# First stages of a two-layer state-space and attention kernel: a new order of the work, and row means by TensorE from transposed rows

## The chip, the cores and the metric

The kernel runs on one core of a Trainium2 chip. Its time is device microseconds (us) of that core. Five engines work side by side, each through its own instructions in order: PE (TensorE, matmuls; PEld is its weight loads), DVE (VectorE), ACT (ScalarE), POOL (GpSimd) and SP (SyncE, which here only issues DMAs). POOL and ACT issue DMAs too. Engines wait for one another, and for DMAs, through semaphores. An instruction that waits holds up all that stand behind it on its engine, DMA issues included.

## The reference

The input u (2048 rows of 512) passes through four blocks: a long convolution (A), a local attention (B), A again and B again, each on the normalised input, and with the input added.

```python
def _A_ref(u, A_re, A_im, B_re, B_im, C_re, C_im, log_dt, Dskip):
    dt = jnp.exp(log_dt)[:, None]
    P = jnp.exp((dt * A)[:, :, None] * l[None, None, :])
    K = jnp.einsum("dn,dnl,dn->dl", Cc, P, dB).real
    ...
    Yf = Uf * Kf[None, :, :, :]
    y = irfft2(Yf)[:, :, 0, :L].transpose + u * Dskip
...
x = A_u
x = x + _A_ref(_layernorm(x, axis=-1), ...)
x = x + _B_ref(_layernorm(x, axis=-1), B_wqkv, B_wo)
x = x + _A_ref(_layernorm(x, axis=-1), ...)
x = x + _B_ref(_layernorm(x, axis=-1), B_wqkv, B_wo)
```

`_layernorm` takes mean and variance of each row of 512. The kernel K of the convolution (2048 lags for each of 512 channels, from 128 modes) and its spectrum are the same in both A blocks and are computed once.

## The kernel before

`kgen` (L384) makes the kernel's spectrum, normalises the rows for the first time, makes the first stage of their transform, and runs the first convolution. All of it is written as small steps with names, and the string `KGEN` (L353) is the order in which they are issued, by hand: each engine gets its instructions in that order. `words` holds each step with the steps that it needs. The part behind the colon, or the first digit, is the quarter of the channels (0 to 3). The steps:

- q, m, l, b (L425 to L441): the ladder. Each rung squares the modes' decay factor (q on ACT, m and l on DVE), and b casts it to bf16 on ACT. x0 to x5 form C times B, and t loads an activation table.
- U and v (`step`, L460): products of table entries with ladder rungs, on DVE. Their pairs are added either on DVE (% steps, L510) or by PE with identity weights (+, `sum_pe`, L521) and a copy on ACT (=, `sum_out`, L531). u, A and B copy start values.
- p (`product`, L558): PE multiplies the two tables of a quarter into lags of the kernel. k (L575) copies them to SBUF, and after the second copy sends them to DRAM and back in another layout (`rows`).
- s (`spectrum`, L593): PE multiplies rows with the transform matrix G. G0 serves parts 0 and 1, G1 parts 2 and 3. o and e (L613, L627) take the result out on ACT and DVE and store it to `kt_scratch` in DRAM, two DMAs of 128 KB each.
- n (`first_norm_row`, L176): sums of one row group of X. On ACT (an a behind the number) that is a pass for the mean (L184) and a pass for the squares (L185). On DVE it is L179 to L181. r and a make scale and bias for eight groups, and N applies them, on ACT (with a, L202) or DVE (L204).
- f (`first_stage`, L633) is the first transform stage of a group on PE with the matrix F1, and z (L638) copies it to Z: whole on ACT, or real and imaginary halves on ACT and DVE.
- c0 to c2 (L660): the last lag. c1 is eight small matmuls on PE and the last reader of the ladder's powers. `C["powers_used"]` holds it.
- w and W with a number of columns (`warm`, L550): matmuls of the identity whose results nobody reads, as filler on PE.
- steps with @: the first convolution, 16 groups (`a_steps`, L211): T transposes on PE, t (or a) copies them on DVE (or ACT), X second stage, c copy on ACT, p (pab, DVE) the product with the spectrum tile Kt, v inverse on PE, V (or W) the copy on ACT (or DVE), k the load of a Kt. U and Y belong to the last lag. A d, q, i, I or J is the second half of the last group.

Kt has five buffers, of two halves of 256 KB each. What the steps behind T0 need from DRAM is placed by `tc.issue_after`: the load of F1T, the matrix of the output stage, right behind `C["powers_used"]`, and the first four Kt loads right behind the steps in `FIRST_LOADS`: two on POOL's queue, behind the last `rows` DMA, and two on SP's queue. `load_b_weights` (L149) also sets a tile `never` to zero on POOL (L152), in memory that G0 held, so it waits for the last read of G0.

X is loaded by four DMAs of 512 KB on SP; F1 (1 MB), G1 (1.5 MB) and then G0 (1.5 MB) follow on the same queue.

Of the kernel before, what the change touches and what calls it, by code (L numbers as in the profile page):

```python
# [11 lines left out]
ACT = mybir.ActivationFunctionType  # L12
# [163 lines left out]
def first_norm_row(nc, small, st, Xg, j, on_act):  # L176
# [7 lines left out]
    nc.scalar.activation(junk[:], x, ACT.Identity, scale=1.0 / D, accum_out=mv[:, 0:1])  # L184
# [131 lines left out]
def a_layer(nc, tc, C, Xg, Ng, kt_dram, layer, Z, es_z, a=None):  # L316
# [10 lines left out]
    def y_rows(g, hf, row, ps, add):  # L327
# [25 lines left out]
KGEN = ("m0 q0 b0 x1 l0 m1 q1 x0 t l1 b1 x3 x2 q2 m2 b2 l2 x5 m3 U4p:1 q3 U4:0 l3 b3 %U4:0 u:1 m4 q4 u:0 l4 b4 m5 q5 U2p:0 l5 +U2p:0 b5 "  # L353
# [30 lines left out]
def kgen(nc, tc, C, prm, kt_dram, Zf, norm_row, norm_rstd, norm_apply, norm_apply_row, norm_tiles, load_rest, es_a, es_y, open_conv):  # L384
    everything = KGEN.split()
    with ExitStack() as es:
# [32 lines left out]
        nc.sync.dma_start(Gt[1][:], C["G_h"].ap()[1])  # L419
# [89 lines left out]

        def sum_dve(name, c):  # L510
            prod, out, hn, f, size = sums[name, c]
            for r in range(2):
                x, y = (prod[i][:, (r + i) % 2].rearrange("n (h f c) -> n h f c", h=hn, f=f) for i in range(2))
                nc.vector.tensor_tensor(out(r), x, y, ALU.add if r else ALU.subtract)
# [6 lines left out]
        def sum_pe(name, c, rs):  # L521
            prod, out, hn, f, size = sums[name, c]
            ps = tiles["+", name, c, rs] = psum()[1].tile([128, 2, 512], F32, name="psadd", tag="psg")
# [16 lines left out]
        def product_tile(c, q):  # L540
            if ("p", c, q // 2) not in tiles:
                tiles["p", c, q // 2] = psum()[0].tile([128, 16, 64], F32, name="psk", tag="psk")
            return tiles["p", c, q // 2]

        def spectrum_tile(c, i):
            if ("s", c, i) not in tiles:
                tiles["s", c, i] = psum()[1].tile([128, 2, 512], F32, name="psg", tag="psg")
            return tiles["s", c, i]

        def warm(tile, cols):  # L550

            flat = tile[:].rearrange("n a b -> n (a b)")
            while cols > 0:
                n = min(cols, 512)
                nc.tensor.matmul(flat[:, 0:n], C["ident"][:], C["ident"][:].unsqueeze(1).to_broadcast([128, n // 128, 128]), start=True, stop=True)
                cols -= n
# [18 lines left out]
        def product_out(c, m):  # L575
# [3 lines left out]
            nc.scalar.copy(KT[:, :, :, m * 16:(m + 1) * 16, :].rearrange("v w t h f -> v (w t) h f"),  # L579
# [5 lines left out]
            for t in range(2):  # L585
                for b in range(2):
# [4 lines left out]
                                                   C["rows_dram"].ap()[c].rearrange("t b w v x -> (w v) (t b) x"))  # L591

# [1136 lines left out]
```

## Time and profile before

| | us |
|---|---|
| median of 3 runs | 423.86 (423.78 to 424.48) |
| the profiled execution's own time | 424.25 |
| its span, from the first to the last instruction | 422.4 |
| DVE busy in the span | 398.4 (94%) |
| PE busy in the span | 379.3 (90%) |
| ACT busy in the span | 332.7 (79%) |
| start of the second layer's norm transposes (pt_x, L1190), after the first convolution | 162.3 |

Times in rows of the profile are from the span's start. A row of the timeline gives start, length, engine, line, operation, output and inputs, shape, and in brackets how long the engine stood idle and what released it. SPq and POOL rows with DMA_DIRECT2D are the issues of transfers, not the transfers. A group's row gives its count, busy time, mean of one in ns and the idle time before. PE's ends are modelled. The granted clock is a share of PE's full speed.

### The profile page before, as it was taken

What the parts mean: (1) busy time and instruction counts of PE and PEld (TensorE: products, weight loads), DVE (VectorE), ACT (ScalarE), POOL (GpSimd) and SP (SyncE); (2) the same over time, 40 slices, a digit from 0 to 9 for tenths busy, and PEclk for the clock granted to TensorE, in tenths of its full rate; (3) what the DMA queues carried; (4) which work ended last, traced back from release to release, by engine and by line L of the source; (5) the groups of instructions that cost most, each with busy time, mean ns of one, the idle gap of its engine ahead of it and who ended that gap; (6) DMA issues with size and microseconds to landing.
All of it is one profiled execution on the core that took longest, in us unless ns stands there. A gap on an engine that the chain in (4) does not pass through costs nothing.

```text
span 422.4 us, 12235 instructions
## 1 busy us (share of the span) xinstructions
PE 379.3 (90%) x5120; PEld 259.1 (61%) x5120; DVE 398.4 (94%) x730; ACT 332.7 (79%) x600; POOL 26.0 (6%) x68
## 2 busy tenths in 40 slices
PE   1157898999989999999999999889999999997996
PEld 1023585676458755587866575278855686875663
DVE  5999999999889979899999999999989999999994
ACT  6999998998979989766665699989988676663542
POOL 5000011001210000002020000000000001200000
PEclk9999999999999999999999999999999999998999
DMA  8900001254889960005480028239300009350022
GB/s 241 424 29 0 2 12 42 76 166 104 250 245 276 259 213 2 2 2 98 81 174 3 2 64 238 102 107 288 107 0 4 2 2 166 73 115 2 2 102 101
DMA packets 25822, 44.09 MB, mean 104 GB/s; under 512 B 7317, under 2 KB 17238, under 8 KB 25126
## 3 DMA queue, kind: packets, MB, share of 16 engines
q1 hardware_dynamic: 22918, 38.09, 31.9%
q0 software_dynamic: 1888, 4.56, 5.0%
q8 instruction: 40, 0.66, 0.6%
q10 hardware_dynamic: 960, 0.66, 0.5%
q14 instruction: 16, 0.13, 0.1%
HBM read 29.04 MB, written 6.95 MB: 85 GB/s over the span
## 4 chain that ended last, share of the span: by engine, by line
PE 46%; DVE 25%; ACT 7%; DMA 6%; issue 4%; SPq 2%; DVEq 0%; ACTq 0%
PE ps_qk L1207 10%; DVE prodpv L1403 9%; PE ps_v L1294 5%; DVE prodqk L1257 4%; PE vp L291 3%; PE psg L601 3%; PE Lp L1279 3%; PE po L1413 3%; PE ps_o L1443 2%; DVE Z L504 2%; DVE pab L275 2%; DMA Kt<-kt_scratch 2%; PE psk L568 2%; DMA V<-V 2%; ACT Z L1496 2%
## 5 line engine op out<-in xcount | busy, mean ns | idle before, releaser
L1403 DVE TENSOR_TENSOR prodpv<-V,Lsb 128x2048 bf16<-128x2048 bf16 x64 | 75.3, 1221 | 0.7 <-DMA V<-V 0.4
L1207 PE MATMUL ps_qk<-xnT,wqk 128*128 128x512 bf16 x256 | 59.9, 379 | 0.0
L1255 DVE TENSOR_TENSOR prodqk<-qT,N 128x1024 bf16<-128x1024 bf16 (+3 forms) x88 | 42.6, 544 | 1.9 <-ACT N L1210 1.9
L1257 DVE TENSOR_TENSOR prodqk<-qT,N 128x1024 bf16<-128x1024 bf16 (+3 forms) x56 | 40.4, 765 | 0.3 <-ACT qT L1210 0.2
L1413 PEld LDWEIGHTS <-prodpv 128*128 128x128 bf16 x1024 | 35.3, 100 | 7.2 <-DVE prodpv L1403 2.0
L275 DVE TENSOR_TENSOR pab<-xc,Kt 128x2048 bf16<-128x2048 bf16 (+1 forms) x34 | 38.8, 1154 | 0.7 <-issue 0.4
L1413 PE MATMUL po<-halves,prodpv 128*128 128x64 bf16 x1024 | 38.1, 196 | 0.9 <-DVE prodpv L1403 0.9
L1207 PEld LDWEIGHTS <-wqk 128*128 128x128 bf16 x256 | 23.7, 98 | 23.5
L269 ACT CAST xc<-xp 128x1024 bf16<-128x1024 f32 (+1 forms) x34 | 34.6, 1033 | 2.2 <-PE xp L263 1.9
L291 PEld LDWEIGHTS <-pab 128*128 128x128 bf16 x512 | 30.4, 98 | 7.0 <-DVE pab L275 3.5
L291 PE MATMUL vp<-sb_IC,pab 128*128 128x128 bf16 x512 | 33.6, 219 | 0.6 <-DVE pab L275 0.3
L1279 PEld LDWEIGHTS <-prodqk 128*128 128x128 bf16 x1024 | 29.8, 96 | 5.5 <-DVE prodqk L1257 2.5
L295 ACT CAST VT<-vp 128x1024 bf16<-128x1024 f32 (+1 forms) x31 | 32.7, 1065 | 0.6 <-PE vp L291 0.6
L1443 PE MATMUL ps_o<-wo_t,oT 128*128 128x512 bf16 x128 | 33.0, 379 | 0.0
L1279 PE MATMUL Lp<-sb_bones,prodqk 128*128 128x8 bf16 x1024 | 30.5, 166 | 1.0 <-DVE prodqk L1257 0.8
L528 PE MATMUL psadd<-Z,sb_ident 128*128 128x384 bf16 (+3 forms) x75 | 18.7, 337 | 13.1 <-DVE Z L504 7.9
L1294 PE MATMUL ps_v<-wv,xnT 128*128 128x256 bf16 x256 | 30.4, 272 | 0.0
L1424 ACT CAST oT<-po 128x512 bf16<-128x512 f32 x32 | 17.7, 589 | 13.8 <-PE po L1413 13.7
L1210 ACT CAST N<-ps_qk 128x512 bf16<-128x512 f32 x32 | 18.7, 587 | 12.1 <-PE ps_qk L1207 11.9
L1160 DVE BATCH_NORM_STATS2 ln_stats<-X 128x6 f32<-128x512 bf16 x39 | 24.9, 682 | 2.7 <-ACT X L1549 2.7
L1301 ACT CAST V<-ps_v 128x512 bf16<-128x512 f32 x32 | 18.2, 588 | 10.9 <-PE ps_v L1294 10.8
L1294 PEld LDWEIGHTS <-xnT 128*128 128x128 bf16 x256 | 24.2, 98 | 3.2
(202 smaller groups left out, 837.8 us busy)
## 6 DMA issues: line engine op xcount, KB each, us to landing
Kt<-kt_scratch SPq DMA_DIRECT2D x60, 256.0 KB, 5.5
kt_scratch<-ks SPq DMA_DIRECT2D x32, 128.0 KB, 3.0
G<-c_G SPq DMA_DIRECT2D x2, 1536.0 KB
V<-V SPq DMA_DIRECT2D x8, 288.0 KB, 7.8
X<-in_A_u_dram SPq DMA_DIRECT2D x4, 512.0 KB, 4.8
F1Tsb<-c_F1T SPq DMA_DIRECT2D x2, 1024.0 KB
V<-V SPq DMA_DIRECT2D x4, 512.0 KB
V<-V POOLq DMA_DIRECT2D x4, 384.0 KB, 8.3
```

Of the source, the lines that this page charges most:

```text
L269: nc.scalar.copy(xcs[cg][:, gs].rearrange("q g o l -> q (g o l)"), xps[cg][:].rearrange("q h n -> q (h n)")[:, gs.start * 128:gs.stop * 128])
L275: nc.vector.tensor_tensor(pabs[cg][:, gs], xcs[cg][:, gs].to_broadcast([128, gs.stop - gs.start, 2, 128]), kts[cg][:, gs], ALU.mult)
L291: a.last_pe = nc.tensor.matmul(vp[:, g, :], pabs[cg][:, gs.start + g, ab, :], C["IC"][:, ab, :], start=(ab == 0), stop=(ab == 1))
L295: copy(dst[..., parts(cg)[part]], vps.pop((cg, part))[:].rearrange("k g (q e) -> k q e g", e=GE))
L1207: nc.tensor.matmul(t.ps[:], wqk[:, ct, f0:f0 + 128], x_group(g)[:, :, ct], start=(ct == 0), stop=(ct == 3))
L1255: nc.vector.tensor_tensor(b.pr[:, u:u + 2 * n, 1 - halves_of[0], :], q, cols(kT[i][:, starts[0]:starts[0] + n * 128]), ALU.mult)
L1257: nc.vector.tensor_tensor(b.pr[:, u:u + 2 * n].rearrange("f u a q -> f a u q")[:, ::-1], q.unsqueeze(1).to_broadcast([128, 2, 2 * n, 64]), ...
L1279: nc.tensor.matmul(t.Lp[:, w, u % 2, u // 2, :], b.pr[:, u].rearrange("f a q -> f (a q)"), bones[:], start=False, stop=(t.parts == W // 2 ...
L1294: nc.tensor.matmul(t.ps[:, jj, :], tokens(ct, jp * 2 + jj, c), wv[:, ct, fp * 256:(fp + 1) * 256], start=(jj + ct == 0), stop=(jj == 1 and ...
L1403: nc.vector.tensor_tensor(t.p2[:, c:c + k, 0:nj, :].rearrange("p c j (d h) -> p c j d h", d=DH), m.V2[i // 2][:, c0 + c:c0 + c + k, r0:r0 ...
L1413: nc.tensor.matmul(po[jj // k][:, jj % k, c, :], t.p2[:, c - c0, jj, :], fold, start=(first and c == c0 and jj % k == 0), stop=(last and c ...
L1443: nc.tensor.matmul(t["ps"][:], m.oT[:, ft, j * 128:(j + 1) * 128], wo_t[:, ft, :], start=(start and ft == lo), stop=(ft == 3 or kept and f ...
```

## The change

It has four parts.

1. The order `KGEN` is replaced from its first step to its last. The same work is in it, with these differences: row group 2 is summed on ACT (n2a for n2); 13 groups are normalised on ACT and 3 on DVE (8 and 8 before); other groups' z are split; t3 runs on DVE instead of ACT, and V8 is W8 (DVE); the filler has 9,088 columns in six places (14,720 in twelve before). F1T and the first Kt loads are placed by the same rules as before. c0 now stands some ten steps ahead of the end of the spectrum, and c1 right behind its last tile, s31.
2. The means: X is transposed by 16 DMAs on SP's queue, right behind its loads, into the memory of G1 (groups 0 to 11) and F1 (12 to 15). The step xm sums over the transposed rows with 64 matmuls by a column of ones, and xo scales the sums into the means on ACT. The ACT pass for the mean (L184) is gone, and all n, f and s steps need xo. G1 and F1 are loaded behind xo's place, ahead of G0 on SP.
3. The filler is given with a number of columns alone (~) and goes ahead of the next tile that PE opens.
4. A k step may go to DVE, and a z half to either engine; the new order uses the second only.

```diff
     junk = small.tile([128, D], BF, name="n1_junk", tag="junk", bufs=1)
-    nc.scalar.activation(junk[:], x, ACT.Identity, scale=1.0 / D, accum_out=mv[:, 0:1])
     nc.scalar.activation(junk[:], x, ACT.Square, scale=-1.0, bias=mv[:, 0:1], accum_out=st["m2"][:, j:j + 1])
...
-KGEN = ("m0 q0 b0 x1 l0 m1 q1 x0 t l1 b1 x3 x2 q2 m2 b2 l2 x5 m3 U4p:1 q3 U4:0 l3 b3 %U4:0 u:1 m4 q4 u:0 l4 b4 m5 q5 U2p:0 l5 +U2p:0 b5 "
...
-        "U256p:0 =v4p:1 %U256:1 Ba:0 +U256p:0 w03:384 l9 =U1p:1 b10 v8p:0 =U256p:0 w03:1536 +0v8p:0 U1024p:1 Ba:1 +1v8p:0 U1024p:0 "
...
-        "q10 %U512:0 n3a =0v8p:1 U512p:1 w03:6144 p03 n9a v16xn:0 p02 n14a +0U512p:1 +1U512p:1 v16x:1 n0a n2 =1U512p:1 l10 prep p00 n4a "
...
-        "s30 z15 f13 e33 f2 z13a z13v z2a z2v s31 o30 @T0 @k4 @T1 @t0 o31 e31 @t1 @X0 @c0 @T2 @t2 @T3 @p0 @k5 @X1 @T4 @c1 @X2 @a3 @c2 e30 "
+KGEN = ("q0 m0 b0 t x0 l0 q1 b1 x1 m1 l1 x3 x2 q2 b2 m2 l2 m3 x5 U4p:1 U4:0 +U4p:1 u:0 q3 l3 b3 =U4p:1 q4 u:1 m4 %U4:0 l4 b4 q5 U2p:0 m5 v2p:0 "
...
+        "l7 b8 v4p:0 U1p:1 U256:1 q8 m8 l8 ~1408 +v4p:0 +U1p:1 =v4p:0 =U1p:1 b7 q9 Ba:0 +v4p:1 xm U256p:0 m9 %U256:1 l9 =v4p:1 b10 xo +U256p:0 "
...
+        "=U1024p:1 n3a q10 U512:0 l10 %U512:0 v16xn:0 +1v8p:1 +0v8p:1 prep n9a n14a n0a n4a =0v8p:1 =1v8p:1 ~3712 p03 p02 p01 U512p:1 +0U512p:1 "
...
+        "z40a f9 z9 s30 o30 f10 z100a f11 z101v z11 s31 c1 o31 c2 @T0 @T1 e30 @t0 @t1 @X0 @T2 @T3 e31 @k4 @t2 @t3 @c0 @X1 @c1 @p0 @k5 @T4 @T5 "
...
         load_rest()
-        nc.sync.dma_start(Gt[1][:], C["G_h"].ap()[1])
+        flat = [Gt[1][:].rearrange("n a b -> n (a b)"), C["F1"][:].rearrange("n a b c -> n (a b c)")]
+        xT = [flat[j // 12][:, j % 12 * D:(j % 12 + 1) * D].rearrange("n (t p) -> n t p", t=4) for j in range(NJ)]
+        for j in range(NJ):
+            nc.sync.dma_start_transpose(xT[j], C["x_row"](j))
...
+        def fresh(tile):
+            warm(tile, late.pop("fill", 0))
+            return tile
...
+        def row_sums():
+
+            ps = tiles["m"] = fresh(psum()[1].tile([128, 2, 512], F32, name="psm", tag="psg"))
+            for j in range(NJ):
+                for t in range(4):
+                    nc.tensor.matmul(ps[:, 0, j:j + 1], xT[j][:, t, :], C["signs"][:, 0:1], start=(j + t == 0), stop=(j == NJ - 1 and t == 3))
+
+        def row_sums_out():
+            nc.scalar.activation(C["mean"](), tiles["m"][:, 0, 0:NJ], ACT.Copy, scale=1.0 / D)
+            nc.sync.dma_start(Gt[1][:], C["G_h"].ap()[1])
+            nc.sync.dma_start(C["F1"][:], C["F1_h"].ap())
+        word("xm", row_sums, "x5")
+        word("xo", row_sums_out, "xm")
...
-            word(f"n{j}", lambda j=j: norm_row(j, False))
-            word(f"n{j}a", lambda j=j: norm_row(j, True))
+            word(f"n{j}", lambda j=j: norm_row(j, False), "xo")
+            word(f"n{j}a", lambda j=j: norm_row(j, True), "xo")
...
-            if full[0] in "wW":
-                word(full, lambda full=full: warm((product_tile if full[0] == "w" else spectrum_tile)(int(full[1]), int(full[2])), int(full.split(":")[1])), "x5")
+            if full[0] == "~":
+                word(full, lambda full=full: late.update(fill=int(full[1:])))
...
         Xg.extend(load_x(nc, late, A_u[0]))
-        nc.sync.dma_start(C["F1"][:], C["F1_h"].ap())
```

The issue order on SP's queue that follows from it, around the end of the spectrum. Before: ten stores of the spectrum, F1T, two `rows_scratch` issues, four stores, two more `rows_scratch`, ten stores, and then Kt issues and stores in turn (1 Kt, 2 stores, 1 Kt, 2 stores, 4 Kt, 2 stores, 2 Kt, 2 stores, 20 Kt). After: the last 12 stores ahead of F1T, F1T, 1 store, 4 Kt, 3 stores, 24 Kt. On POOL's queue the memset of `never` stood behind the four Kt issues before, and stands ahead of them after.

More of the change, by code (lines that the diff above doesn't have):

```diff
@@ L508, in step, with warm @@
                 C["powers_used"] = last
+        def warm(tile, cols):
+            flat = tile[:].rearrange("n a b -> n (a b)")
+            while cols > 0:
+                n = min(cols, 512)
+                nc.tensor.matmul(flat[:, 0:n], C["ident"][:], C["ident"][:].unsqueeze(1).to_broadcast([128, n // 128, 128]), start=True, stop=True)
+                cols -= n
+        def fresh(tile):
+            warm(tile, late.pop("fill", 0))
+            return tile
         def sum_dve(name, c):
@@ L522, in sum_pe @@
             prod, out, hn, f, size = sums[name, c]
-            ps = tiles["+", name, c, rs] = psum()[1].tile([128, 2, 512], F32, name="psadd", tag="psg")
+            ps = tiles["+", name, c, rs] = fresh(psum()[1].tile([128, 2, 512], F32, name="psadd", tag="psg"))
             for i in range(2):
@@ L541, in product_tile @@
             if ("p", c, q // 2) not in tiles:
-                tiles["p", c, q // 2] = psum()[0].tile([128, 16, 64], F32, name="psk", tag="psk")
+                tiles["p", c, q // 2] = fresh(psum()[0].tile([128, 16, 64], F32, name="psk", tag="psk"))
             return tiles["p", c, q // 2]
@@ L546, in spectrum_tile @@
             if ("s", c, i) not in tiles:
-                tiles["s", c, i] = psum()[1].tile([128, 2, 512], F32, name="psg", tag="psg")
+                tiles["s", c, i] = fresh(psum()[1].tile([128, 2, 512], F32, name="psg", tag="psg"))
             return tiles["s", c, i]
[L550 to L556, printed above, removed]
         def product(c, q):
@@ L633, in first_stage @@
         def first_stage(j):
-            ps = tiles["f", j] = psum()[0].tile([128, 2, D], F32, name="ps_s1", tag="psk")
+            ps = tiles["f", j] = fresh(psum()[0].tile([128, 2, D], F32, name="ps_s1", tag="psk"))
             for r in range(2):
@@ L639, in first_stage_out @@
             src = tiles["f", j][:].rearrange("k r (c e g) -> k r c g e", c=16, e=GE)
[L640 to L644 removed]
+            if not part:
                 nc.scalar.copy(C["z_view"][:, :, j], src)
+                return
+            r = int(part[0])
+            (nc.scalar.copy if part[1] == "a" else nc.vector.tensor_copy)(C["z_view"][:, r, j], src[:, r])
         word("y", lambda: nc.scalar.copy(Ln[:], lads[7][:, 1, :]), "l6")
@@ L725, in kgen @@
             for m in range(2):
-                word(f"k{c}{m}", lambda c=c, m=m: product_out(c, m), f"p{c}{2 * m}", f"p{c}{2 * m + 1}", "prep")
+                for v, copy in (("", nc.scalar.copy), ("v", nc.vector.tensor_copy)):
+                    word(f"k{c}{m}{v}", lambda c=c, m=m, copy=copy: product_out(c, m, copy), f"p{c}{2 * m}", f"p{c}{2 * m + 1}", "prep")
             for i in range(4):
-                word(f"s{c}{i}", lambda c=c, i=i: spectrum(c, i), f"k{c}0", f"k{c}1")
+                word(f"s{c}{i}", lambda c=c, i=i: spectrum(c, i), *[w for w in everything if w.rstrip("v") in (f"k{c}0", f"k{c}1")], "xo")
                 word(f"o{c}{i}", lambda c=c, i=i: spectrum_odd(c, i), f"s{c}{i}")
@@ L1656 @@
     n1 = {}
+    C["x_row"] = lambda j: Xg[j // 4][:, j % 4, :]
+    C["mean"] = lambda: n1["st"]["mv"][:, :, 0]
     def load_rest():
```

13 lines of the change are left out of this document (4 added, 9 removed), and 27 rows, old and new, of the table KGEN.

## The prediction

> **What bounds the kernel now.** I read the busy time of each engine by stage first, then the queue rows around the stage that the change reorders, then the groups of instructions. The stages are cut at three rows of the timeline: the first product matmul, the last spectrum tile (the end of s31, called S below: 117.85 + 1.46 = 119.31), and the last wait of the first convolution.
>
> ```profile
> 49.26 0.40 PE L568 MATMUL psk<-Utab,Vtab 128*64 128x40 bf16 x8 [0.20 <-DVE Utab L514]
> 117.85 1.46 PE L606 MATMUL psg<-G,rows 128*128 128x512 bf16 x6
> 150.37 1.29 DVE L275 TENSOR_TENSOR pab<-xc,Kt 128x1024 bf16<-128x1024 bf16 x2 [0.34 <-DMA Kt<-kt_scratch]
> ```
>
> ```profile
> 0.00:49.26 49.26, 23.11 (x114) 11.35 (x115) 44.16 (x92) 44.19 (x75) 6.24 (x28) 0.97 0.41 149
> 49.26:119.31 70.05, 67.89 (x1056) 46.12 (x1055) 66.93 (x132) 64.37 (x129) 9.54 (x16) 1.00 0.38 107
> 99.33:119.31 19.98, 19.44 (x142) 9.88 (x140) 17.04 (x31) 17.18 (x26) 3.90 (x7) 1.00 0.69 197
> 119.31:151.66 32.35, 29.92 (x408) 24.41 (x408) 30.82 (x38) 30.21 (x35) 1.26 (x8) 1.00 0.99 274
> 130.00:146.00 16.00, 16.00 (x227) 13.30 (x226) 15.99 (x19) 16.00 (x18) 0.00 (x0) 1.00 1.00 267
> ```
>
> The columns are stretch, length, busy time of PE, weight loads, DVE, ACT and POOL, granted clock, DMA share, GB/s. Up to the first product, DVE and ACT are both full. From there to S, PE has the least left over: 70.05 - 67.89 = 2.16 us idle, against 3.12 on DVE and 5.68 on ACT. In the convolution all three are nearly full, and so are the DMA engines: 0.99 of their time, 1.00 between 130 and 146 us, where little moves but the spectrum tiles Kt. At its end DVE waits 0.34 us for the last Kt. So the convolution runs exactly as long as its Kt loads need, although these have a head start:
>
> ```profile
> 107.45 2.03 POOL L230 DMA_DIRECT2D Kt<-kt_scratch  x4 [0.35 <-DVE N L204]
> 119.37 0.53 POOL L152 MEMSET never<- 128x512 bf16 x1 [9.89 <-PE psg L606]
> 89.92 0.44 SPq L233 DMA_DIRECT2D F1Tsb<-c_F1T  x1
> 113.91 0.57 SPq L230 DMA_DIRECT2D Kt<-kt_scratch  x1
> 126.52 17.90 SPq L230 DMA_DIRECT2D Kt<-kt_scratch  x20
> Kt<-kt_scratch SPq DMA_DIRECT2D x28, 256.0 KB, 5.3
> Kt<-kt_scratch POOLq DMA_DIRECT2D x4, 256.0 KB, 5.7
> kt_scratch<-ks SPq DMA_DIRECT2D x18, 128.0 KB, 1.9
> F1Tsb<-c_F1T SPq DMA_DIRECT2D x2, 1024.0 KB
> ```
>
> The first four Kt issues stand on POOL 11.9 us ahead of S, and F1T went at 89.92, when DMA had room. The memset of `never` comes after them on POOL, where nobody waits for it.
>
> **The change part by part.** *Engine work.* The rows:
>
> ```profile
> L184 ACT ACTIVATE n_junk<-X 128x512 bf16<-128x512 bf16 x15 | 9.5, 636 | 0.1
> L184 ACT ACTIVATION_READ_ACCUMULATOR n_junk<-X 128x1 f32 x15 | 3.0, 198 | 0.0
> L185 ACT ACTIVATE n_junk<-X,n_mv 128x512 bf16<-128x512 bf16 x15 | 10.8, 723 | 0.5
> L185 ACT ACTIVATION_READ_ACCUMULATOR n_junk<-X,n_mv 128x1 f32 x15 | 2.8, 188 | 0.0
> L202 ACT ACTIVATE N<-X,n_nb,n_rstd 128x512 bf16<-128x512 bf16 x8 | 6.3, 809 | 0.0
> L204 DVE TENSOR_SCALAR N<-X,n_rstd,n_nb 128x512 bf16<-128x512 bf16 x8 | 2.9, 418 | 0.0
> L179 DVE BATCH_NORM_STATS2 n_stats<-X 128x6 f32<-128x512 bf16 x1 | 0.7, 718 | 0.0
> L254 ACT COPY zt<-pt 128x1024 bf16<-128x1024 bf16 x1 | 1.0, 1019 | 0.0
> L254 DVE COPY zt<-pt 128x1024 bf16<-128x1024 bf16 x15 | 10.1, 684 | 0.8 <-PE pt L248 0.8
> L295 ACT CAST VT<-vp 128x1024 bf16<-128x1024 f32 x15 | 16.6, 1107 | 0.2 <-PE vp L291 0.2
> L295 DVE CAST VT<-vp 128x512 bf16<-128x512 f32 x1 | 0.7, 671 | 0.0
> ```
>
> ACT loses the 15 mean passes (9.5 + 3.0 = 12.5 us). It gains the squares of row 2 (0.72 + 0.19) and five row normalisations (13 instead of 8, 5 x 0.81 = 4.05), and the small copy of the means, which costs more than nothing and less than 0.6, a 512-column row's time; I take 0.2. Up to S that is -7.3 us. DVE loses row 2's statistics (0.72 and two small operations; the statistics alone bound it from below, I take 1.0) and five normalisations (5 x 0.42 = 2.1): -3.1. In the convolution one transposed copy and one inverse copy go from ACT (-1.02 - 1.11) to DVE (+0.68, and for 1024 columns up to twice 0.67). The z copies stay eight whole and sixteen half ones.
>
> *PE* gets 64 matmuls of one column, and loses filler: 14,720 columns become 9,088.
>
> ```profile
> L1279 PE MATMUL Lp<-sb_bones,prodqk 128*128 128x8 bf16 x1024 | 30.5, 166 | 1.0 <-DVE prodqk L1257 0.8
> L555 PE MATMUL psk<-sb_ident 128*128 128x512 bf16 x13 | 3.0, 379 | 0.0
> 37.26 0.59 PE L528 MATMUL psadd<-Z,sb_ident 128*128 128x512 bf16 x2 [0.63 <-DVE Z L504]
> 4.22 2.21 SPq L144 DMA_DIRECT2D X<-in_A_u_dram  x4
> X<-in_A_u_dram SPq DMA_DIRECT2D x4, 512.0 KB, 4.8
> 69.55 2.37 PE psg L601 x10
> ```
>
> The nearest row to the 64 matmuls, with a weight load each, is L1279: 30.5 / 1024 = 30 ns, so 1.9 us. The 5,632 columns less save 5,632 x 3.0 / 6,656 = 2.5 us. Both lie ahead of 49.26, but for a few hundred columns, and PE idles 26 us there: nothing. Without that cover, 1.9 us would fall on the sums behind xm on PE and on the ACT copies that wait for them.
>
> *The transposes* (2.1 MB, queued on SP behind X) must be done before PE reaches xm, ahead of the sums of U256p:0, which PE reached at 37.26: by 37.26 - 1.9 = 35.4. X has landed by 4.22 + 2.21 + 4.8 = 11.2. No row shows a transpose. As plain copies at 267 GB/s they take 7.9 us (done at 19); one after another, at 1.9 us for each 128 KB as the stores have, 16 take 30.4 (done at 41.6, 6.2 late). I take the first, because the four X loads show that this queue overlaps its transfers: nothing. G1, F1 and G0 now load behind xm on SP, 4.2 MB, about 16 us at 267 GB/s, so by about 53. Their first user is s01, as the first spectrum tile, which ran at 69.55.
>
> *By pages alone:* the Trainium skill's "Advanced Engine Details and Errata", section "X-Bar Transpose (TRN2)", has transposes as fast as plain copies, 350 to 400 GB/s, which would give an estimate of 5 to 6 us. The Trainium skill's "VectorE: DVE Perf Modes", section "The three transpose paths", has 1,309 ns for 128x128, which for 64 blocks end to end would be an estimate of 84 us. No run here shows either.
>
> *Up to S.* ACT's 7.3 us aren't worth 7.3, for PE is in the way: its work after 49.26 is the same but for the eight matmuls of the last lag (c1). The gain lies between 0 and DVE's limit, its idle time before S and its saved work: (19.98 - 17.04) + 3.1 = 6.0. I take PE's whole idle time, **2.2**.
>
> *The queues.* The order puts c1 directly behind s31, and the load of F1T is tied to the last use of the powers, which c1 now is. So on SP's queue F1T waits for S, and behind it stand one store, the first four Kt issues on that queue, three stores and the other 24 Kt. On POOL's queue the memset of `never`, which waits for s31 (the G0 tile), now precedes all four Kt issues. So no Kt starts before S, where the rows above have five half tiles issued by 114, and F1T's 1 MB falls into the same stretch. Behind the late Kt waits pab of group 0 on DVE, and behind that DVE's copies of T4 and on.
>
> From S: the memset 0.06 + 0.53, one issue 2.03 / 4 = 0.51, start-up 1.4 (1.9 to landing less 0.5 for 128 KB at 267 GB/s): 2.5 us. Then the 28 + 4 issues of 256 KB, 8.39 MB of Kt, and four stores, 0.52 MB, at 267 GB/s: 33.4; F1T's 1.05 MB at the rate of the long rows early in the kernel: 2.5.
>
> ```profile
> 14.00:20.00 6.00, 1.21 (x8) 0.69 (x8) 5.67 (x13) 5.99 (x8) 0.00 (x0) 1.00 1.02 428
> 122.00:125.00 3.00, 2.19 (x24) 1.48 (x23) 2.98 (x5) 2.32 (x3) 0.00 (x0) 1.00 0.95 292
> 140.00:143.00 3.00, 3.00 (x47) 2.59 (x44) 3.00 (x4) 3.00 (x4) 0.00 (x0) 1.00 1.03 257
> ```
>
> So the last Kt is there at S + 2.5 + 33.4 + 2.5 = S + 38.4; before, DVE's wait for it ended at 150.37 = S + 31.1. **+7.3 us.** At 292 GB/s it is +4.4; at 257, with F1T no faster than Kt, +10.2. DVE's extra copies, about 2 us, hide in that wait, and ACT's relief too; without it DVE would be the bound and they would show.
>
> **Sum:** -2.2 + 7.3 = +5.1 on the profiled 424.25, which is 0.39 above the median of the runs, 423.86. So **428.9**. Its own range is 424.2 (+4.4, with S halfway to DVE's limit, -4.1) to 433 (+10.2, with S gaining half of 2.2).
>
> **The rivals.** *The Kt loads stay hidden.* If DMA can go faster than its full rows show, or the prefetch of five tiles covers the late start, the convolution keeps its 32.35 us and S moves up: 423.86 - 2.2 = 421.7, down to 417.8 if DVE is the only bound. For it: a wait of only 0.34 us is charged to Kt now. Against: no stretch behind S shows that rate, and the share is 1.00 over 16 us. It takes over where the 9.96 MB need under 30.8 us (31.1 + 2.2 - 2.5), above 323 GB/s. *The transposes come late.* PE stands at xm, and the sums, their copies, every square and the reload of the tables stand behind it. One after another: 6.2 us late, 428.9 + 6.2 = 435.1; from there each us later is one more. Against: overlap of the X loads. Beside it, the Trainium skill's 1,309 ns would make it about 60 us. *Both cancel*: a gain of 6 before S against +6 behind it, 423.9.
>
> **How the numbers follow.** Forecast 0.66 (424.2 to 433); Kt hidden 0.18; transposes late 0.10; cancelled 0.06. Faster by over 0.2% (about what can be told from no change here, 0.85 us) is the hidden case and a tail of the cancelled one, 0.20; within 0.2%, 0.07; slower 0.73. The range 421 to 434 leaves out the lower half of the hidden case and most of the late transposes.
>
> **What would show it.** Right: F1T and the first Kt issued behind the last spectrum matmul; a DMA share of 1.0 from S until the last pab; DVE waits for Kt of some 7 us in the convolution, which is near 40 us long from S (38.4 and the last pab's 1.29); S near 117; PE without a wait at xm. Wrong: S later than 119 with PE waiting for DMA at 35 us; a convolution stage still near 32 us; or a PE clock below 1.00 after 49 us for want of filler (it reads 1.00 there now).

## The result, and the profile after

The changed kernel takes 436.52 us (median of 6 runs, 434.31 to 437.65), against 424.03 us (6 runs, 422.43 to 424.50) for the kernel before beside it: 1.0286 times as long, 95% interval 1.0259 to 1.0313. The prediction was 428.9, with a range of 421 to 434. The direction was right; the size was not, and the time lies outside the range. One execution in this document, of c_early at 431.45 us, counts as slow; it is in that kernel's median and not in its ratio.

The stages of the profiled execution after, cut at the same three rows as before. First the rows of the timeline at the cuts (the last two rows are the end of the last pab), then the table by stretch (columns as in the prediction: stretch, length, busy time of PE, weight loads, DVE, ACT and POOL, granted clock, DMA share, GB/s).

```profile
49.64 0.40 PE L573 MATMUL psk<-Utab,Vtab 128*64 128x40 bf16 x8 [0.56 <-DVE Utab L527]
121.27 1.46 PE L625 MATMUL psg<-G,rows 128*128 128x512 bf16 x6
160.28 1.23 DVE L274 TENSOR_TENSOR pab<-xc,Kt 128x2048 bf16<-128x2048 bf16 x1 [0.25 <-DMA Kt<-kt_scratch]
162.25 1.29 DVE L274 TENSOR_TENSOR pab<-xc,Kt 128x1024 bf16<-128x1024 bf16 x2 [0.74 <-DMA Kt<-kt_scratch]
```

```profile
0.00:49.64 49.64, 23.52 (x163) 12.18 (x166) 44.34 (x93) 44.16 (x76) 6.26 (x28) 0.97 0.67 190
49.64:122.73 73.09, 67.46 (x1044) 45.94 (x1050) 64.66 (x124) 58.63 (x106) 7.49 (x12) 0.98 0.26 70
122.73:163.54 40.81, 32.38 (x410) 25.95 (x416) 32.37 (x39) 30.10 (x34) 3.24 (x12) 0.96 0.99 279
68.70:72.10 3.40, 3.40 (x9) 1.17 (x9) 1.43 (x5) 0.53 (x1) 1.12 (x2) 0.50 0.24 48
```

| | before | after | difference | predicted |
|---|---|---|---|---|
| first product | 49.26 | 49.64 | +0.38 | 0 |
| from there to S | 70.05 | 73.09 | +3.04 | -2.2 |
| from S to the last pab | 32.35 | 40.81 | +8.46 | +7.3 |
| the rest of the profiled time (424.25 and 436.82) | 272.59 | 273.28 | +0.69 | 0 |

The relief of ACT is there (58.63 us busy between the first product and S, 64.37 before) and DVE has less to do too, yet the stage is longer. What the prediction had not counted is that PE now has 73.09 - 67.46 = 5.63 us idle, against 2.16, and that its clock is no longer granted in full: 0.50 from 68.7 to 72.1. This is the timeline of the changed kernel around that place.

```profile
59.46 0.69 ACT L584 CAST KT<-psk 128x640 bf16<-128x640 f32 x1 [0.74 <-PE psk L573]
60.44 1.13 POOL L592 DMA_DIRECT2D rows_scratch<-KT  x2 [15.32 <-ACT KT L584]
64.53 0.77 POOL L595 DMA_DIRECT2D rows<-rows_scratch  x1 [2.95 <-DMA rows_scratch<-KT]
68.23 4.04 PE L620 MATMUL psg<-G,rows 128*128 128x512 bf16 x9 [1.29 <-DMA rows<-rows_scratch]
72.31 1.01 ACT L636 CAST ks<-psg 128x1024 bf16<-128x1024 f32 x1 [3.07 <-PE psg L620]
73.37 0.59 PE L541 MATMUL psadd<-Z,sb_ident 128*128 128x512 bf16 x2 [0.88 <-ACT ks L636]
73.78 0.49 DVE L497 TENSOR_TENSOR Z<-cb,Z 128x256 bf16<-128x256 bf16 x2 [3.65 <-PE psadd L541]
```

The lags of the first quarter are copied by 60.15, go to DRAM and come back as rows at 68.2: 8.1 us. In the new order PE reaches s01 1.29 us before that. It stands, and what stands behind s01 in its order (the sums of quarters 2 and 3) stands with it. The s01 matmuls then take 4.04 us where ten of them took 2.37 before. ACT waits 3.07 us for their result and DVE 3.65 us for the sums behind them. At the last quarter's rows (s32, at 114.83) PE waits another 0.92 us for such a trip. In the kernel before, the trip of the first quarter was as long (61.44 to 69.55, 8.1 us), but two sums stood ahead of s01 on PE (68.21 to 69.55, behind a wait of 0.91 us for DVE), and its weight loads stood 0.49 us for the rows. The timeline of before (the first and the last row of the two sums, and the weight loads of s01):

```profile
60.77 0.67 ACT L579 CAST KT<-psk 128x640 bf16<-128x640 f32 x1
68.21 0.27 PE L528 MATMUL psadd<-Z,sb_ident 128*128 128x128 bf16 x2 [0.91 <-DVE Z L496]
69.17 0.38 PE L528 MATMUL psadd<-Z,sb_ident 128*128 128x512 bf16 x1
69.55 1.88 PEld L601 LDWEIGHTS <-rows 128*128 128x128 bf16 x10 [0.49 <-DMA rows<-rows_scratch]
```

The end of the spectrum and the start of the convolution, from the timeline of the changed kernel:

```profile
122.79 0.53 POOL L152 MEMSET never<- 128x512 bf16 x1 [11.30 <-PE psg L625]
123.33 0.33 SPq L232 DMA_DIRECT2D F1Tsb<-c_F1T  x1
123.42 0.53 POOL L229 DMA_DIRECT2D Kt<-kt_scratch  x1
124.19 2.66 SPq L229 DMA_DIRECT2D Kt<-kt_scratch  x4
132.16 1.22 DVE L274 TENSOR_TENSOR pab<-xc,Kt 128x2048 bf16<-128x2048 bf16 x1 [3.94 <-DMA Kt<-kt_scratch]
133.44 1.83 PE L290 MATMUL vp<-sb_IC,pab 128*128 128x128 bf16 x16 [3.55 <-DVE pab L274]
135.68 1.22 DVE L274 TENSOR_TENSOR pab<-xc,Kt 128x2048 bf16<-128x2048 bf16 x1 [1.69 <-DMA Kt<-kt_scratch]
```

This is as predicted: the memset first, then F1T and the first Kt on both queues, none of them ahead of S. The DMA share is 0.99 over the whole stage. DVE waits for Kt four times, 3.94 + 1.69 + 0.25 + 0.74 = 6.6 us in all. The granted clock is 0.96 over this stage, because it is half from 133.5 to 137.0; that cost nothing that can be told: s01_fill and order_only, below, have some 7 us of half clock in the convolution (130.5 to 137.5 and 138.5 to 145.5), and those stages aren't longer than this one.

The transposes, which no row showed before (timeline of the changed kernel):

```profile
9.45 15.70 SPq L420 DMA_TRANSPOSE G<-X  x12
25.20 5.30 SPq L420 DMA_TRANSPOSE F1sb<-X  x4
35.02 1.34 PE L603 MATMUL psm<-signs,G 128*128 128x1 bf16 x48 [0.21 <-issue]
36.22 0.54 PE L603 MATMUL psm<-signs,F1sb 128*128 128x1 bf16 x16
```

They take (15.70 + 5.30) / 16 = 1.31 us of SP's queue each. The issue of the last begins at 29.2 and its data is there 2.5 us later, at 31.7, some 3 us ahead of xm, which doesn't wait. They were not late.

### The profile page after: what moved, and what is told of

It reads as the page before. It is cut to its first block, busy times and chain, and to the rows that moved or that the text cites. A ratio compares the mean times of both kernels' runs of the same rounds, so it can differ in the third digit from the quotient of the medians.

```text
span 434.9 us, 12284 instructions
## 1 busy us (share of the span) xinstructions
PE 379.0 (87%) x5132; PEld 259.7 (60%) x5172; DVE 397.8 (91%) x724; ACT 326.3 (75%) x576; POOL 25.9 (6%) x68
## 4 chain that ended last, share of the span: by engine, by line
PE 32%; DVE 21%; DMA 8%; ACT 5%; issue 4%; SPq 0%; DVEq 0%; ACTq 0%
DVE prodpv L1422 11%; PE ps_qk L1226 8%; DVE prodqk L1276 6%; DMA Kt<-kt_scratch 6%; PE ps_v L1313 3%; PE vp L290 3%; PE Lp L1298 3%; PE ps_o L1462 2%; PE po L1432 2%; DMA V<-V 2%; ACT Z L1515 2%; DVE pab L274 2%; PE ps_y L343 2%; PE pt_x L1209 2%; PE ps_y L338 2%
## 5 line engine op out<-in xcount | busy, mean ns | idle before, releaser
L268 ACT CAST xc<-xp 128x1024 bf16<-128x1024 f32 (+1 forms) x34 | 33.4, 995 | 9.7 <-DVE pab L274 5.2
L1432 PEld LDWEIGHTS <-prodpv 128*128 128x128 bf16 x1024 | 34.0, 98 | 8.2 <-DVE prodpv L1422 2.9
L1432 PE MATMUL po<-halves,prodpv 128*128 128x64 bf16 x1024 | 37.0, 193 | 1.8 <-DVE prodpv L1422 1.7
L1462 PE MATMUL ps_o<-wo_t,oT 128*128 128x512 bf16 x123 | 32.0, 379 | 0.4
L294 ACT CAST VT<-vp 128x1024 bf16<-128x1024 f32 (+1 forms) x30 | 30.5, 1029 | 1.9 <-DMA Kt<-kt_scratch 0.9
L541 PE MATMUL psadd<-Z,sb_ident 128*128 128x256 bf16 (+3 forms) x72 | 18.6, 338 | 11.1 <-DVE Z L505 3.9
```

The lines of the kernel that those rows point to most:

```text
L268: nc.scalar.copy(xcs[cg][:, gs].rearrange("q g o l -> q (g o l)"), xps[cg][:].rearrange("q h n -> q (h n)")[:, gs.start * 128:gs.stop * 128])
L294: copy(dst[..., parts(cg)[part]], vps.pop((cg, part))[:].rearrange("k g (q e) -> k q e g", e=GE))
L1432: nc.tensor.matmul(po[jj // k][:, jj % k, c, :], t.p2[:, c - c0, jj, :], fold, start=(first and c == c0 and jj % k == 0), stop=(last and c ...
L1462: nc.tensor.matmul(t["ps"][:], m.oT[:, ft, j * 128:(j + 1) * 128], wo_t[:, ft, :], start=(start and ft == lo), stop=(ft == 3 or kept and f ...
```

## The experiments

Theory after these rows: the 8.5 us behind S are the loads that wait for c1 and for the memset; the 3.0 us ahead of it are PE's stand at s01 and the half clock behind it. The rivals: that the new order of the convolution itself is slower; that the loss ahead of S is spread over the order; that the transposes or the later loads cost something. Ratios are to the kernel before, run beside each.

| kernel | median us | ratio (95% interval) | first product | to S | S to last pab |
|---|---|---|---|---|---|
| c_early | 426.98 | 1.0059 (1.0032 to 1.0086) | 50.50 | 71.08 | 32.07 |
| never_behind | 431.03 | 1.0192 (1.0155 to 1.0230) | 49.70 | 73.60 | 36.30 |
| f1t_late | 431.80 | 1.0238 (1.0176 to 1.0301) | 50.21 | 71.64 | 36.15 |
| s01_late | 436.59 | 1.0294 (1.0249 to 1.0339) | 50.49 | 72.34 | 40.54 |
| s01_fill | 434.14 | 1.0234 (1.0197 to 1.0272) | 49.97 | 71.90 | 39.84 |
| s01_behind | 425.54 | 1.0059 (1.0036 to 1.0082) | 49.51 | 70.53 | 32.24 |
| means_only | 425.47 | 1.0020 (0.9990 to 1.0050) | 49.70 | 69.83 | 31.65 |
| order_only | 441.67 | 1.0424 (1.0368 to 1.0481) | 50.76 | 78.35 | 39.49 |
| p3_early | 430.72 | 1.0184 (1.0159 to 1.0210) | 50.25 | 75.27 | 32.20 |
| fill_more | 426.02 | 1.0049 (1.0028 to 1.0070) | 49.54 | 70.43 | 32.08 |
| rows3_later | 426.09 | 1.0057 (1.0037 to 1.0076) | 49.68 | 71.01 | 32.76 |
| tr_twice | 453.32 | 1.0716 (1.0673 to 1.0759) | 66.14 | 71.15 | 40.57 |

The three stage columns are from one profiled execution each. How much such an execution can be off is seen where the edit doesn't touch a stage: behind S, the changed kernel, s01_late, s01_fill, order_only and tr_twice, which hold the same loads back, have 39.49 to 40.81 us, and the five of the new order with F1T and Kt as before have 32.07 to 32.76.

### c_early: the last lag where it was

```diff
-... p00 ... k01 =1U512p:1 k00 v16yn:1 ... =1v8p:2 =0v8p:2 %v4:3 ... o02 U256:3 ... e33 c0 z40a ... s31 c1 o31 c2 @T0
+... p00 ... k01 =1U512p:1 k00 c0 v16yn:1 ... =1v8p:2 =0v8p:2 c1 %v4:3 ... o02 c2 U256:3 ... e33 z40a ... s31 o31 @T0
```

> The changed kernel with c0, c1 and c2 (the last lag) moved back to where the old order had them; F1T then goes on SP's queue ten stores earlier than the last rows_scratch issues, and all four Kt issues stand on POOL ahead of the memset of never. Theory (F1T and Kt held behind S cost the convolution 8.5 us): S stays at 122.7 within 0.7, the convolution stage falls from 40.8 to 32 to 33.5, the time is 8 us less, 428.5 (427.5 to 429.5). Rival 1 (the new order of the convolution's own steps costs it, and the late loads are only what the profile names): the stage stays above 36, the time above 432. Rival 2 (the late loads are one half and the late c2, on which T0 waits, and the half clock at 133.5 the other): 34 to 36, 430 to 432.

The stage behind S is 32.07 us, as the theory has it, and the first rival falls. The second (half for the late c2 and the half clock) falls by its numbers only, since this run moves c2 as well; what settles it are never_behind and f1t_late, below. The table by stretch of this run:

```profile
50.50:121.58 71.08, 66.30 (x1049) 46.05 (x1055) 64.56 (x124) 59.22 (x107) 9.51 (x16) 1.00 0.39 110
121.58:153.65 32.07, 29.08 (x402) 24.57 (x408) 31.89 (x39) 28.13 (x33) 1.25 (x8) 1.00 0.95 274
```

In the second row DVE is busy 31.89 of 32.07 us: with Kt early again, DVE bounds the convolution, and its extra copies show (30.82 before). The stage ahead of S moved too, which was not expected, so that the time, 426.98, lies below the expected 427.5 to 429.5. In its timeline the rows happened to be back in time, and the clock stayed at 1.00:

```profile
67.97 2.35 PE L620 MATMUL psg<-G,rows 128*128 128x512 bf16 x9 [0.17 <-DMA rows<-rows_scratch]
```

### never_behind and f1t_late: which load is worth what

never_behind is the changed kernel with only the memset behind the Kt issues of POOL's queue. f1t_late is c_early with only F1T late.

```diff
-    nc.gpsimd.memset(C["never"][:], 0.0)
...
+    def clear():
+        nc.gpsimd.memset(C["never"][:], 0.0)
...
+    C["clear"] = clear
...
         with tc.issue_after(C[FIRST_LOADS[cg]].ins) if layer == 0 else nullcontext():
             load_k(cg, ...)
+        if layer == 0 and cg == 1:
+            with tc.issue_after(C["kt_load"].ins):
+                C["clear"]()
```

> The changed kernel with one edit: the memset of never is issued on POOL behind the four Kt issues of that queue, as before; SP's queue is unchanged, with F1T and 28 Kt issues behind c1. So 1 MB of Kt may be fetched ahead of S. If the convolution's length is the bytes that are left behind S at the full rate (267 GB/s): 1.05 MB less is 3.9 us, the stage 36.9, the time 432.6. If it is the first Kt alone that matters (pab of group 0 waits 3.9 us, PE then runs at half clock, and what follows keeps up): the stage falls to 33 to 34, the time 429. If the memset holds nothing that F1T and the SP issues don't hold as well: 40 or more, the time 436.

```diff
-    if layer == 0:
-        with tc.issue_after(C["powers_used"].ins):
-            load_f1t()
...
             eng.dma_start(kts[cg][h::2]..., rows)
+        if layer == 0 and cg == 4:
+            load_f1t()
```

> The kernel of c_early with one edit: F1T (1.05 MB) is issued on SP behind the two issues of @k4, so just behind S, while the first Kt stay early. By the bytes behind S: 2.5 us (at 428 GB/s) to 3.9 us (at 267) more than c_early, a stage of 34.6 to 36, 429.5 to 431 in time. If DMA has slack in c_early (share 0.95, DVE 31.9 of 32.1 us busy): about 1.6 us of it is free, a stage of 33 to 34.4. If F1T costs nothing there: 32.

Both came out near what the bytes left behind S give, never_behind somewhat below it (a stage of 36.9 and 432.6 expected), f1t_late somewhat above (at most 36 and 431). In never_behind, the timeline and the table by stretch show four Kt issues ahead of S and a stage 4.51 us shorter than the changed kernel's:

```profile
112.09 2.02 POOL L232 DMA_DIRECT2D Kt<-kt_scratch  x4
123.36 0.52 POOL L154 MEMSET never<- 128x512 bf16 x1 [9.25 <-PE psg L631]
```

```profile
123.30:159.60 36.30, 31.19 (x416) 24.89 (x416) 32.16 (x39) 29.99 (x34) 1.25 (x8) 1.00 0.98 278
```

In f1t_late F1T alone makes the stage 36.15 - 32.07 = 4.08 us longer, which is 1.05 MB at 257 GB/s, and the wait for Kt is back (table and timeline):

```profile
121.85:158.00 36.15, 29.96 (x408) 24.44 (x408) 32.05 (x39) 28.43 (x33) 1.26 (x8) 1.00 0.93 272
```

```profile
137.53 1.22 DVE L273 TENSOR_TENSOR pab<-xc,Kt 128x2048 bf16<-128x2048 bf16 x1 [3.59 <-DMA Kt<-kt_scratch]
```

4.51 + 4.08 = 8.59, and c_early undid 8.74. So the term is accounted for by the two holds, about half each, and little (0.15 us, within the spread) is left for the late c2, which never_behind still has.

### s01_fill, s01_late and s01_behind: the stand at s01

```diff
-... U1024:2 ua:3 s01 N2a o01 +v2p:3 +U1p:2 =v2p:3 n12a =U1p:2 N4a ...
+s01_fill:   ... U1024:2 ua:3 ~3072 s01 N2a o01 +v2p:3 +U1p:2 =v2p:3 n12a =U1p:2 N4a ...
+s01_late:   ... U1024:2 ua:3 N2a +v2p:3 +U1p:2 s01 =v2p:3 o01 n12a =U1p:2 N4a ...
+s01_behind: ... U1024:2 ua:3 +v2p:3 +U1p:2 =v2p:3 s01 =U1p:2 N2a o01 n12a N4a ...   (on c_early)
```

> The changed kernel with 3,072 columns of filler ahead of s01 (six matmuls of 512, some 1.3 us), which fill PE's wait for the rows; s01 is not earlier by it. If half of the loss at s01 is the clock (3.4 us at 0.5, so 1.7 us): granted clock 1.00 from 66 to 74, S 1.5 to 2 us earlier, the time 434.5 to 435. If it is the latency of the rows alone, or if the filler pushes s01 back: S unchanged or up to 0.3 later, 436.5. If the clock is throttled for another reason than the idle stretch ahead of it, it stays 0.5 there.

> The changed kernel with one edit: s01 stands behind the sums +v2p:3 and +U1p:2 on PE, not ahead of them, and o01 behind =v2p:3. Theory (PE, in its order, stands at s01 for the rows that are not back from DRAM, and then runs at half clock): no wait of PE for rows over 0.5 us at 66 to 70, granted clock 1.00 there, S 3 to 3.5 us earlier, about 119.5, the time 433 (432.5 to 434). Rival (the 3.5 us are the sum of several small waits, of which this is the visible one): S no more than 1 us earlier, 435.5 or more.

> The kernel of c_early with s01 behind the sums +v2p:3 and +U1p:2 on PE, as in s01_late, but also =v2p:3 ahead of N2a on ACT, so that s01 doesn't stand for a buffer of the sums either. In s01_late s01 began at 70.45, behind 1.10 us of wait for that copy, and S was no earlier than in the changed kernel, though the clock was granted in full. If only that wait kept it: s01 at 69 to 69.5, no half clock at 66 to 74, S 1 us earlier than in c_early, the time 426 (425 to 426.5). If the sums' copies and squares on ACT and the products on DVE wait for one another whichever stands first: S within 0.4 of c_early, 427.

The rows of PE's timeline in the three, in this order:

```profile
69.25 2.35 PE L620 MATMUL psg<-G,rows 128*128 128x512 bf16 x9 [0.58 <-DMA rows<-rows_scratch]
```

```profile
70.45 2.32 PE L620 MATMUL psg<-G,rows 128*128 128x512 bf16 x10 [1.10 <-ACT Vtab L551]
```

```profile
68.80 2.32 PE L620 MATMUL psg<-G,rows 128*128 128x512 bf16 x10 [0.41 <-ACT Vtab L551]
```

With filler the clock stayed at 1.00 there, and the stage to S fell from 73.09 to 71.90 us, although s01 began later than in the changed kernel (69.25, not 68.23). That puts some 1.2 us on the clock, less than the 1.5 to 2 expected. The time is 2.2 us less by the ratios; the other half is the stage behind S, 39.84 against 40.81, which lies within the spread of that stage. s01_late came out as its rival had it (S at 122.83, 436.59 us), but it doesn't show what the rival says: N2a stood ahead of =v2p:3 on ACT, so that s01 now stood for that copy; one wait took the place of another, and the time is that of the changed kernel. With N2a behind (s01_behind) the stage is 70.53 us, 0.55 less than c_early; 1 us was expected. The ratios of c_early and s01_behind are the same, 1.0059, so the total doesn't tell these two apart.

Two runs more show the price of the clock with the same wait ahead of it. f1t_late and tr_twice (below) stood at s01 as long as the changed kernel (f1t_late first):

```profile
68.81 2.35 PE L619 MATMUL psg<-G,rows 128*128 128x512 bf16 x10 [1.30 <-DMA rows<-rows_scratch]
```

```profile
84.67 2.35 PE L620 MATMUL psg<-G,rows 128*128 128x512 bf16 x10 [1.24 <-DMA rows<-rows_scratch]
```

Their clock stayed at 1.00 there. The stage of f1t_late is 71.64 us against 73.09 with the half clock: 1.45 us. (Its c0 and c1 stand elsewhere, though, as in c_early.) That of tr_twice, which has the changed kernel's order and only comes 16.5 us later, is 71.15: 1.94 us. The wait by itself shows less: c_early, with 0.17 us of it, has 71.08, which is 0.56 less than f1t_late and 0.07 less than tr_twice. So of the two, the half clock is the larger part, 1.2 to 1.9 us.

### means_only and order_only: the two halves of the change

means_only is the kernel before in its own order, with xm ahead of U256p:0, xo behind b10, and the transposes and later loads. order_only is the changed kernel with the pass for the means back on ACT, no transposes, and F1 and G1 loaded right behind X.

```diff
-KGEN of the change
+KGEN of before: "... q9 +U1p:1 ~128 xm U256p:0 ... =U1p:1 b10 xo v8p:0 ..."
```

> The kernel before, in its own order, with the means by TensorE alone: 16 transposes on SP, xm ahead of U256p:0, xo behind b10, G1 and F1 loaded behind xo, filler as before. Theory of the prediction (ACT is not the bound of 49 to 119 us, PE is): S moves by 0 to -2.2, the convolution stays at 32.4, the time is 422 to 424. Rival 1 (ACT's relief is worth more, as it is full up to the first product): first product earlier than 48 or S earlier than 117, 421 or less. Rival 2 (the transposes, 21 us on the queue, or the later load of G1 and F1 come late): PE waits at xm or s01, over 424.7.

```diff
-        for j in range(NJ):
-            nc.sync.dma_start_transpose(xT[j], C["x_row"](j))
+        nc.sync.dma_start(Gt[1][:], C["G_h"].ap()[1])
...
+    nc.scalar.activation(junk[:], x, ACT.Identity, scale=1.0 / D, accum_out=mv[:, 0:1])
...
-        word("xm", row_sums, "x5")
-        word("xo", row_sums_out, "xm")
+        word("xm", lambda: None, "x5")
+        word("xo", lambda: None, "xm")
```

> The changed kernel with the old means: the pass of 512 columns for each of the 16 groups is back on ACT (16 x 0.83, 13.4 us), there are no transposes, xm and xo do nothing, and F1 and G1 are loaded right behind X. If ACT's relief is what the new order lives on: ACT's idle 14.5 us between the first product and S are used up, S 2 to 5 us later, the time 438.5 to 441.5. If the path to S runs over PE, DVE and the trips through DRAM, and ACT's idle time was at the same places as the passes: S within 1 us, the time 436 to 437.5. If the transposes or the later loads cost the changed kernel something: earlier, under 435.5.

In the old order the means by TensorE are worth nothing that can be told: 1.0020, interval 0.9990 to 1.0050. The time, 425.47, lies above the expected 422 to 424 and where the second rival had it (over 424.7), but that rival's sign is missing: PE waits neither at xm nor, for rows, at s01. In the profiled execution (426.62) all up to the last pab is 0.5 us shorter than in the kernel before, and what follows, which the edit doesn't touch, 2.9 us longer (275.44 against 272.59); why is open. The table by stretch shows where ACT's relief went. ACT is 10 us less busy than before in this stage, and the stage is 0.22 us shorter:

```profile
49.70:119.53 69.83, 67.05 (x1048) 46.07 (x1055) 66.91 (x132) 54.28 (x101) 9.51 (x16) 1.00 0.40 114
```

In the new order the same relief seems worth more: 441.67 - 436.52 = 5.2 us (5.9 by the ratios, 1.0424 and 1.0286, whose intervals are 0.3 to 0.6% wide to each side). The stage up to S shows it, 78.35 us against 73.09. There the sums of the rows stand among the copies of the first quarter's lags: in order_only's timeline PE stands 2.56 us for the copy of KT that is queued behind these passes on ACT, and the granted clock is half from 63.5 to 77.5.

```profile
63.13 0.40 PE L571 MATMUL psk<-Utab,Vtab 128*64 128x40 bf16 x8 [2.56 <-ACT KT L582]
```

So the new order with the means left on ACT loses some 18 us (441.67 against 423.50), and the means by TensorE give 5 or 6 of them back.

### tr_twice: what a transpose costs

```diff
-        for j in range(NJ):
+        for j in [*range(NJ), *range(NJ)]:
             nc.sync.dma_start_transpose(xT[j], C["x_row"](j))
```

> The changed kernel with the 16 transposes issued twice, to the same places. In the changed kernel they take 1.31 us of SP's queue each, the last is there at about 33 and xm runs at 35. If transposes go one behind the other at 1.31 us: 21 us more, xm at 54 to 55 and everything behind it late, the time 19 us or so longer, 455. If the issue time is what the queue needs but the transfers overlap: the same here. If the second pass runs at the rate of plain copies (7.9 us): xm at 41 to 43, the time 442 to 444.

They come one every 1.31 us, as the first expectation had it. PE, now waiting for each second transpose, shows it (two of 16 such rows), and the first sum behind xm starts at 54.57, as expected; the time is 453.32, 16.8 us more than the changed kernel's, where some 19 were expected. Whether the 1.31 us are the issue on SP or the transfer, the runs don't separate; with 2.5 us from issue to landing, one is issued before the one ahead of it has landed.

```profile
36.65 0.25 PE L603 MATMUL psm<-signs,G 128*128 128x1 bf16 x4 [1.06 <-DMA G<-X]
37.95 0.26 PE L603 MATMUL psm<-signs,G 128*128 128x1 bf16 x4 [1.05 <-DMA G<-X]
```

### p3_early, fill_more and rows3_later: attempts to beat both

p3_early is c_early, fill_more is s01_behind, rows3_later is fill_more, each with one edit:

```diff
-p3_early:    ... k30 o13 z2 s00 f0 z00v z01a o00 p33 p32 f12 e13 e00 s23 k31 ...
+             ... k30 o13 p33 p32 z2 s00 f0 k31 z00v z01a o00 f12 e13 e00 s23 ...
-fill_more:   ... +v4p:1 xm U256p:0 ...
+             ... +v4p:1 ~3072 xm U256p:0 ...
-rows3_later: ... s32 z31a z15 o32 f6 z61v ...
+             ... z31a f6 s32 z15 o32 z61v ...
```

> The kernel of c_early with one edit: p33 and p32 stand ahead of s00 and f0 on PE, and k31 ahead of z0 on ACT, so that the last quarter's rows leave some 2.5 to 3 us earlier. In c_early PE waits 1.70 us at s32 for these rows. If that wait is on the path to S: S 1.5 us earlier relative to the first product, the time 425.5 (425 to 426). If s00 and z0, now later, take its place, or DVE and ACT wait for each other anyway: S unchanged, 427, or later.

> [...] If the clock ahead of the first product is worth nothing, since DVE and ACT set that time: the first product still at 49.5, the time 425.5. If PE is on that path: no half clock at 37 to 41, the first product up to 0.9 us earlier, the time 424.7. If xm is later by the filler and the squares or the loads of G1 and F1 behind it matter: later.

> The kernel of fill_more with f6 ahead of s32 on PE (and z31a ahead of it on ACT), which fills the 0.85 us for which PE stands at s32 for the last quarter's rows. If that wait is on the path: S 0.5 to 0.8 us earlier from the first product than in fill_more, the time 0.5 to 0.8 less. If DVE's and ACT's copies of the transform set the time there: no change.

p3_early is 4 us slower than c_early. Its rows left earlier, but a spectrum tile stood for DVE instead, and in its profile PE also met the wait at s01 with the half clock behind it (70.0 to 73.5), so that the run doesn't show what the edit alone is worth:

```profile
69.43 3.82 PE L620 MATMUL psg<-G,rows 128*128 128x512 bf16 x10 [1.89 <-DMA rows<-rows_scratch]
108.95 1.24 PE L625 MATMUL psg<-G,rows 128*128 128x512 bf16 x5 [1.54 <-DVE ks L649]
```

fill_more removed the half clock at 37 to 41 and left the first product at 49.54 (49.51 without the filler): these 3.4 us of half clock cost nothing. Some 7 us of it there seem not to be free, though: in four runs that have them in one piece (c_early, f1t_late, s01_late and p3_early, between 36 and 44) the first product starts at 50.21 to 50.50, in six with 3.4 us or none (the changed kernel, never_behind, s01_fill, s01_behind, fill_more and rows3_later) at 49.51 to 49.97, and up to there all ten are the same program but for fill_more's and rows3_later's filler. In rows3_later the wait for rows is gone, and a wait of 1.39 us for ACT's copy of Z stands one instruction earlier; it gains nothing. No version of the new order beat the kernel before; the nearest, c_early, s01_behind, fill_more and rows3_later, are 0.5 to 0.6% slower.

## Why the prediction was wrong in size

**Up to S (-2.2 predicted, +3.0 measured): this is the step that failed.** It makes 5.2 of the 7.5 us by which the profiled time exceeds the sum (436.82 against 424.25 + 5.1). It read "ACT's 7.3 us aren't worth 7.3, for PE is in the way", took PE's whole idle time as the gain, and bounded it by 0 and -6.0. That ACT doesn't hold this stage is borne out by means_only: -0.22 us for 10 us of relief. What failed is the bound at 0. PE's idle time was treated as something that can only go away; but an order written by hand also decides how much idle time there is, and PE's grew from 2.16 to 5.63 us. The new order sends PE to s01 before its rows are back from DRAM, and the clock falls to half behind that wait. Of the 3.0 us, 2.0 are gone where the rows are back in time and the clock is full (c_early, which moves c0 to c2 as well); the clock's share of these is 1.2 (s01_fill) to 1.9 (tr_twice). Another 0.55 goes with s01 behind the sums (s01_behind), and 0.5 is left, whose cause stays open: p3_early and rows3_later only moved waits about. These last two are no larger than what single executions differ by. The listing of the new order had shown s01 ahead of two sums that preceded it before; the 8 us of a trip through DRAM stood in the rows of before. The two were not put side by side.

**The convolution (+7.3 predicted, +8.5 measured): right in mechanism, short in one term.** F1T was sized by the rate of the long rows early in the kernel, 428 GB/s, at 2.5 us. Behind S it shares the full queues with Kt and costs 4.08 us (f1t_late), which was the upper bound's assumption (257 GB/s). That is 1.6 us more, where 1.2 are missing in the term, so the rest of the term was some 0.4 too long. The wait of DVE for Kt, 6.6 us, was put at some 7.

**The transposes (0 predicted, 0 measured): right, for a wrong reason.** They were taken as overlapping, 7.9 us in all, because the X loads overlap. They took 1.31 us each, 21 us in all. They were in time only because the queue had some 3 us to spare, which is luck, and tr_twice shows what 16 more cost. The Trainium skill's "Advanced Engine Details and Errata", section "X-Bar Transpose (TRN2)", has them as fast as plain copies; here, on one queue and with 128 KB each, 2.1 MB in 21 us are 100 GB/s, so the measurement decides against it. The Trainium skill's "VectorE: DVE Perf Modes", section "The three transpose paths", has 1,309 ns for a block of 128x128; here 1.31 us carried a transfer of four such blocks, so the figure agrees for one transfer and not for one block.

**Filler, xm, the copy of the means:** 64 matmuls took about 1.7 us (1.9 predicted), the copy 0.32 (0.2), all hidden as said, and 3,072 columns more of filler win nothing (fill_more). DVE's extra copies showed up as soon as the wait for Kt was gone (c_early), as said.

**The signs given in advance:** of the right ones, the order of the issues, the DMA share, DVE's waits, a stage of about 40 us and PE without a wait at xm came true; S near 117 did not (122.73). Of the wrong ones, a clock below 1.00 behind 49 us came true, but for want of rows, not of filler. S is later than 119, but without PE waiting at 35. The rivals fell: Kt did not stay hidden, the transposes were not late, and the two parts did not cancel, since both are losses. The remaining 1.1 us of the difference (0.38 ahead of the first product, 0.69 behind the last pab) were not looked into.

## What to carry to other kernels

In an order written by hand, look for each trip through DRAM and add up the work that stands on the consuming engine between the copy that starts the trip and the instruction that needs it: less work than the trip takes is a stand of that engine and of all behind it, however busy the profile shows the engine now. An engine's idle time in the profile is no lower bound for its idle time in another order, so the range of a reordering needs a loss in it. A load pushed behind the start of a stage that DMA already fills costs its bytes at that stage's rate, not at the rate that the same load had elsewhere.

## What the hardware showed that was not expected

The half clock comes in stretches of 3.4 us, or of several times that (14 us in order_only), and, near s01, only behind a wait of PE; but the length of the wait alone doesn't decide. Behind waits of 1.29 (the changed kernel), 1.85 (never_behind) and 1.89 us (p3_early) it came, behind 1.24 (tr_twice) and 1.30 us (f1t_late) it did not. The Trainium skill's "TensorE: Matmul & The Clock Gate", section "Part 1: The HAM clock gate (the "warmup" mystery)", names a free-running window of 3,413 ns, which agrees with the length of the stretches and would explain that two like waits end differently; its rule that the clock falls after an idle window of about 3.4 us is not what these rows show, since PE's idle ahead of the half clock was 1.29 us in one piece. What part of such a window must be idle was not tried, and where the windows lie no trace here shows.

The trip of the rows through DRAM, from the end of the second KT copy to the first spectrum matmul, varied from run to run by about as much as the wait at s01: 8.1 us in the changed kernel, 7.0 in c_early (61.01 to 67.97), 8.8 in s01_fill (60.48 to 69.25). So whether PE stands there, and whether the half clock follows, differs between executions of nearly the same program. The executions of c_early alone show as much: 424.71 and 425.46 us at a granted clock of 0.996 over the whole run, 427.58 and 428.62 at 0.983 and 0.984; where in the run these lost it isn't recorded. The differences of a few tenths of a us between these variants shouldn't be read as more than that.
